# GELU MLP forward and backward on one core: a quarter of the slope's columns moved from VectorE to GpSimd in the first block

## Chip, core and metric

The kernel runs on one core of one Trainium2 chip. The metric is the device time of one launch in microseconds. A core has TensorE (matrix products, PE in the profile), VectorE (DVE), ScalarE (ACT), GpSimd (POOL) and SyncE (SP, which here only issues DMAs). TensorE writes its products to PSUM; GpSimd works on SBUF alone here.

## What is computed

A two-layer MLP with the tanh form of GELU, and all its gradients. Shapes: 2048 tokens, D = 448, F = 1792, all bf16.

```python
def _fwd_reference(x, w1, b1, w2, b2):
    h = jnp.einsum("bsd,df->bsf", x, w1) + b1
    h = _gelu(h)                     # jax.nn.gelu(x, approximate=True)
    return jnp.einsum("bsf,fd->bsd", h, w2) + b2

def reference(x, w1, b1, w2, b2, grad_out):
    ...
    _out, _vjp = jax.vjp(_f, x, w1, b1, w2, b2)
    _grads = _vjp(grad_out)
    return (_out0, *[jnp.asarray(_g) for _g in _grads])
```

So there are six outputs: the forward result, and the gradients of x, w1, b1, w2 and b2.

## The kernel before

The work is cut into four blocks of 512 tokens, and each block into 7 steps; a step holds two tiles of 128 hidden columns (f) by 512 tokens, so most tiles are 128 partitions by 2 x 512. Step numbers g run on over the blocks: 0 to 6 are the first block. The order of all instructions is written out by hand (`tc.manual_schedule()`), and each engine takes its instructions in that order.

What one step does, by function:

- `M1` (L251) and `rest` (L262, L266): TensorE makes u = x·w1 for a later step into the PSUM tile x, and begins grad_out·w2ᵀ in the PSUM tile z; `M4` (L272) completes z.
- `act_copy` (L297, L298): ScalarE copies u + b1 to V in SBUF and makes A, its scaled square. `act_gelu` (L301) makes hT = GELU(u).
- `dve_first` (L396): VectorE makes B, the cubic argument of tanh, from A and V. `act_second` (L399): ScalarE makes t = tanh.
- `dve_second`: VectorE makes the slope factor. `dve_p` (L402) makes p = (A + C)·hT; `dve_rest` makes t + 1 (L406), p - 1/2 (L407) and t·(p - 1/2) into t (L408).
- `dve_gate` (L416): VectorE makes ghT = (t + 1)·z, reading z in PSUM.
- `grow` (L437): TensorE adds this step's products to the block's forward output, held in the PSUM tiles y and w.

V, A and B have one buffer each; t and p have two, taken in turn by steps. In the first block the loop is, per step g:

```python
        if g > 0:
            rest([g + 1], [(g, pair("z"))])
            M4(g)
            dve_gate(g)
        if g < NPAIR - 1:
            act_first(g + 1)
            dve_first(g + 1)
            act_second(g + 1)
            dve_second(g + 1)
            grow(g, range(2 if g == 0 else 0, SPB))
            M1(g + 2, pair("x"))
            continue
```

`act_first` is `act_copy` and `act_gelu`. The slope of step 0 is made elsewhere, in two halves, by `first_chain` (its p and p - 1/2 are L359 and L361, with 512 columns). After step 6 the block's forward output is evicted, by ScalarE from y (L464) and by VectorE from w (L466), and the two PSUM tiles go to the next M1 and to the products of the next stage. From step 7 on the steps come in pairs, mixed with longer rows of products (L437).

SP issues the loads. w2ᵀ comes by DMA transposes in pieces of 256 columns; the last piece (`load_w2T(1536, F)`) can't be read with the usual overhang, so it comes in two transposes (L168, L169), and GpSimd copies 64 partitions of it into place (L170); columns 1536 on are first read in step 6. `end_in` does the same for grad_out's last rows, and `load_x` (L162) for those of x. Further, GpSimd issues the DMAs that store hT (L420) and the evicted outputs (L442), and at the end makes two sums over partitions (L602, L613).

Of the kernel before, what the change touches and what calls it, by code (L numbers as in the profile page):

```python
# [9 lines left out]
ALU = mybir.AluOpType  # L10
BF16 = mybir.dt.bfloat16
F32 = mybir.dt.float32

GELU_A = 0.044715
GELU_C = math.sqrt(2.0 / math.pi)
# [3 lines left out]
def kernel(  # L19
# [15 lines left out]
    nc = tc.nc  # L35
    P = 128
    B, S, D = x.shape
    F = w1.shape[1]
# [4 lines left out]
    KF = KD - 1  # L43
    DL = D - KF * P
    DOV = D - P
    DM = KF * P
    SB = 512
    NB = S // SB
    SPB = SB // P
    NPAIR = NF // 2  # L50
# [10 lines left out]
    const = ctx.enter_context(tc.tile_pool(name="const", bufs=1))  # L61
# [9 lines left out]
    def pair(name):  # L71
        return (psum_z if name == "z" else psum_s).tile([P, 2, SB], F32, name=name)
# [17 lines left out]
    B_flat = const.tile([P, 2 * SB], F32, name="Bt")  # L90
    T_flat = const.tile([P, 4 * 2 * SB], BF16, name="T")
    b2_bc = const.tile([P, D], BF16, name="b2_bc")
    b1_col = const.tile([P, NF], F32, name="b1_col")
    w128 = const.tile([P, P], BF16, name="w128")

    w1_sb = w1_flat.rearrange("p (k f) -> p k f", k=KD)
    w2T_sb = w2T_flat.rearrange("p (k f) -> p k f", k=KD)
# [8 lines left out]
    def xq(b):  # L106
        o = (b % 2) * 2 * KD * SB
        return xg_flat[:, o:o + KD * SB].rearrange("p (k s) -> p k s", k=KD)

    def gq(b):  # L110
        o = ((b % 2) * 2 + 1) * KD * SB
        return xg_flat[:, o:o + KD * SB].rearrange("p (k s) -> p k s", k=KD)

    def ring(t, n, g):
        o = (g % n) * 2 * SB
        return t[:, o:o + 2 * SB].rearrange("p (h s) -> p h s", h=2)

    def hT(g):
        return ring(hT_flat, HR, g)
# [7 lines left out]
    def A_of(g):  # L127
        return VA_flat[:, 2 * SB:4 * SB].rearrange("p (h s) -> p h s", h=2)

    def B_of(g):  # L130
        return ring(B_flat, 1, g)

    def t_of(g):
        return ring(T_flat, 4, 2 * (g % 2))

    def p_of(g):
        return ring(T_flat, 4, 2 * (g % 2) + 1)
# [10 lines left out]
    def row0(b):  # L148
        return (b + 1) % NB * SB

    def turn_in(out, src, off):
        nc.sync.dma_start_transpose(out=out, in_=bass.AP(src.tensor, src.offset + off, [src.ap[0], [1, KD * P]]))
# [11 lines left out]
    def end_in(dst, src, wrap):  # L164
        if wrap:
            turn_in(dst, src, 0)
        else:
            nc.sync.dma_start_transpose(out=dst[:, KF, :], in_=src[:, DOV:D])  # L168
            nc.sync.dma_start_transpose(out=dst[:, 0:KF, :], in_=src[:, 0:DM])  # L169
            nc.gpsimd.tensor_copy(out=dst[0:DL, KF, :], in_=dst[DL:P, KF, :])  # L170

    def load_g(b, r0=0, r1=SB):
        end_in(gq(b)[:, :, r0:r1], g2[row0(b) + r0:row0(b) + r1, :], row0(b) + SB < S)

    def load_w2T(f0, f1):
        end_in(w2T_sb[:, :, f0:f1], w2[f0:f1, :], f1 < F)
# [22 lines left out]
    for k in range(7):  # L199
        nc.vector.tensor_scalar(out=number[:, 1 << k:2 << k], in0=number[:, 0:1 << k], scalar1=float(1 << k), scalar2=None,  # L200
                                op0=ALU.add)
    for i in range(P // 32):
        nc.vector.transpose(out=row[32 * i:32 * (i + 1), :], in_=number[0:32, 32 * i:32 * (i + 1)])
    nc.vector.tensor_tensor(out=ident.rearrange("p (a b) -> p a b", b=32), in0=number.rearrange("p (a b) -> p a b", b=32),
                            in1=row[:, None, :].to_broadcast([P, P // 32, 32]), op=ALU.is_equal)
# [6 lines left out]
    load_w2(0, 2)  # L212
    load_w1(nc.sync, 256, 512)
    load_g(0, 0, HB)
    load_g(0, HB, SB)
    load_w1(nc.sync, 512, 768)
    load_w2T(256, 512)
# [22 lines left out]
    def cols(g, h):  # L240
        c = g % NPAIR
        return slice((2 * c + h) * P, (2 * c + h + 1) * P)
# [4 lines left out]
    def M1(g, u, hs=(0, 1)):  # L247
        u_of[g] = [u[:, h, :] for h in range(2)]
        for h in hs:
            for kt in range(KF):  # L250
                nc.tensor.matmul(u_of[g][h], lhsT=w1_sb[:, 1 + kt, cols(g, h)], rhs=xq(g // NPAIR)[:, 1 + kt, :],  # L251
                                 start=(kt == 0), stop=False, skip_group_check=True)

    def rest(us, qs):

        for gg, q in qs:
            g_of[gg] = q
        for i in range(2 * max(len(us), len(qs))):
            n, h = divmod(i, 2)
            if n < len(us):  # L260
                gu = us[n]
                nc.tensor.matmul(u_of[gu][h], lhsT=w1_sb[DL:P, 0, cols(gu, h)], rhs=xq(gu // NPAIR)[DL:P, 0, :],  # L262
                                 start=False, stop=True, tile_position=(DL, 0), skip_group_check=True)
            if n < len(qs):
                gg, q = qs[n]
                nc.tensor.matmul(q[:, h, :], lhsT=w2T_sb[0:DL, KF, cols(gg, h)], rhs=gq(gg // NPAIR)[0:DL, KF, :],  # L266
                                 start=True, stop=False, tile_position=(0, 0), skip_group_check=True)

    def M4(g):
        for h in range(2):  # L270
            for kt in range(KF):
                nc.tensor.matmul(g_of[g][:, h, :], lhsT=w2T_sb[:, kt, cols(g, h)], rhs=gq(g // NPAIR)[:, kt, :],  # L272
                                 start=False, stop=(kt == KF - 1), skip_group_check=True)
# [19 lines left out]
    def act_copy(g):  # L293
        u = u_of.pop(g)
        for h in range(2):
            ft = 2 * (g % NPAIR) + h
            nc.scalar.activation(out=V_of(g)[:, h, :], in_=u[h], func=ACT.Identity, bias=b1_col[:, ft:ft + 1])  # L297
        nc.scalar.activation(out=A_of(g), in_=V_of(g), func=ACT.Square, scale=math.sqrt(3.0 * GELU_C * GELU_A))  # L298

    def act_gelu(g):  # L300
        nc.scalar.activation(out=hT(g), in_=V_of(g), func=ACT.Gelu_apprx_tanh)  # L301

    def act_first(g):
        act_copy(g)
        act_gelu(g)
# [89 lines left out]
    def dve_first(g):  # L395
        nc.vector.scalar_tensor_tensor(out=B_of(g), in0=A_of(g), scalar=3.0 * GELU_C, in1=V_of(g), op0=ALU.add, op1=ALU.mult)  # L396

    def act_second(g):
        nc.scalar.activation(out=t_of(g), in_=B_of(g), func=ACT.Tanh, scale=-1.0 / 3.0)  # L399

    def dve_p(g):
        nc.vector.scalar_tensor_tensor(out=p_of(g), in0=A_of(g), scalar=GELU_C, in1=hT(g), op0=ALU.add, op1=ALU.mult)  # L402


    def dve_rest(g):
        nc.vector.tensor_scalar(out=t_of(g), in0=t_of(g), scalar1=1.0, scalar2=None, op0=ALU.add)  # L406
        nc.vector.tensor_scalar(out=p_of(g), in0=p_of(g), scalar1=-0.5, scalar2=None, op0=ALU.add)  # L407
        nc.vector.tensor_tensor(out=t_of(g), in0=t_of(g), in1=p_of(g), op=ALU.mult)  # L408

    def dve_second(g):  # L410
        dve_p(g)
        dve_rest(g)

    def dve_gate(g):
        q = g_of.pop(g)
        nc.vector.scalar_tensor_tensor(out=ghT(g), in0=t_of(g), scalar=1.0, in1=q[:], op0=ALU.add, op1=ALU.mult)  # L416
# [30 lines left out]
    def grow(g, js):  # L447
        for j in js:
            if g == 0 and j % 2 == 0:
                grown[j] = pair("yw"[j // 2])  # L450
            for h in range(2):
                product(grown[j - j % 2][:, j % 2, 0:D], "o", 0, j, 2 * g + h, j < 2)
# [8 lines left out]
    def evict_two(kind, b, j, t, by_act=False):  # L461
        st = iop.tile([P, 2, D], BF16, name="io_" + kind)
        if kind == "g" or by_act:
            nc.scalar.copy(out=st[:], in_=t[:, :, 0:D])  # L464
        else:
            nc.vector.tensor_tensor(out=st[:], in0=t[:, :, 0:D], in1=b2_bc[:, None, :].to_broadcast([P, 2, D]), op=ALU.add)  # L466
        send(kind, b, j, st)
# [23 lines left out]
    for g in range(NPAIR):  # L491
# [8 lines that stand above are left out]
            dve_second(g + 1)  # L500
            grow(g, range(2 if g == 0 else 0, SPB))
            M1(g + 2, pair("x"))
            continue

        grow(g, range(2))
        for j in range(2):
            nc.tensor.matmul(grown[0][:, j, 0:D], lhsT=w128[:], rhs=b2_bc[:], start=False, stop=True)
        grow(g, range(2, SPB))
        act_copy(g + 1)
        evict_two("o", 0, 0, grown[0], True)  # L510
        act_gelu(g + 1)
        dve_first(g + 1)
        act_second(g + 1)
        dve_p(g + 1)
        evict_two("o", 0, 2, grown[2])
        dve_rest(g + 1)
# [101 lines left out]
    def bank():  # L618
        nonlocal turn
        turn += 1  # L620
        return pair("ywxz"[turn % 4])[:, 0, :]
# [3 lines left out]
    for t0, t1 in ((0, 4), (4, HT)):  # L625
        n = (t1 - t0) * P
        for h in range(2):
            a0, a1 = t0 + h * HT, t1 + h * HT
            cs = slice(a0 * P, a1 * P)
            for kt in range(KF):  # L630
                ps = bank()
# [6 lines left out]
        ps = bank()  # L638
# [6 lines left out]
        for h in range(2):  # L645
            nc.scalar.dma_start(out=out_2[KF * P:D, (t0 + h * HT) * P:(t1 + h * HT) * P],
                                in_=gw1_rem[h * DL:(h + 1) * DL, t0 * P:t1 * P])


    for ft in range(NF):  # L650
        ps = bank()
# [41 lines left out]
```

## Time and profile before

| | us |
|---|---|
| median of three runs | 274.11 (273.96 to 274.13) |
| the profiled execution | 273.92 |
| its span | 272.2 |
| busy in the span: TensorE | 266.2 (98%) |
| VectorE | 193.6 (71%) |
| ScalarE | 143.4 (53%) |
| GpSimd | 53.7 (20%) |

The busy shares are means over stages with different limits. A matmul's end is modelled in the trace, so a busy TensorE can still have been held up. TensorE's granted clock was 1.0 over the whole span. The span is split into 40 equal slices of 6.8 us; in the first block, slices 2 to 7, VectorE shows 8 or 9 tenths busy and GpSimd nearly nothing:

```profile
DVE  5899999989889997889999885399999900000000
ACT  2988889798768677886868760012112121111111
POOL 0000001140513515113030415117000096000000
```

### The profile page before, as it was taken

To read this page: it belongs to the slowest core of one execution; us is meant where nothing else is said; L and a number is where in the kernel's file an instruction comes from. 1 tells how busy PE (TensorE), PEld (TensorE's weight loads), DVE (VectorE), ACT (ScalarE), POOL (GpSimd) and SP (SyncE) were. 2 spreads that over 40 slices of the span, in tenths; PEclk is the share of its full clock that TensorE was granted. 3 is DMA by queue.
4 is the path that set the end of the run, shared out by engine and by line. 5 is a ranking of instruction groups with operands and counts; after the bars stand their busy time and mean duration, and the time that the engine had idled before them with its cause. 6 is when DMAs were issued, how large, how long until landed. Compare 5 with 4: busy or idle time off the path is not lost.

```text
span 272.2 us, 3581 instructions
## 1 busy us (share of the span) xinstructions
PE 266.2 (98%) x1397; PEld 126.9 (47%) x1411; DVE 193.6 (71%) x235; ACT 143.4 (53%) x184; POOL 53.7 (20%) x59
## 2 busy tenths in 40 slices
PE   8999999999999999999999999999999999999995
PEld 3544434544444454444544454554445655555552
DVE  5899999989889997889999885399999900000000
ACT  2988889798768677886868760012112121111111
POOL 0000001140513515113030415117000096000000
PEclk9999999999999999999999999999999999999999
DMA  7999899921729999576332994999999911101110
GB/s 170 197 272 216 156 211 156 268 71 42 215 53 252 182 229 301 139 194 149 78 112 55 237 318 121 300 258 213 166 256 259 192 59 58 53 0 51 53 51 34
DMA packets 100445, 43.52 MB, mean 160 GB/s; under 512 B 89004, under 2 KB 97068, under 8 KB 100428
## 3 DMA queue, kind: packets, MB, share of 16 engines
q1 hardware_dynamic: 93344, 26.65, 51.3%
q0 software_dynamic: 4512, 14.69, 16.4%
q10 hardware_dynamic: 2572, 1.95, 2.3%
q8 instruction: 11, 0.18, 0.3%
q14 instruction: 6, 0.05, 0.1%
HBM read 7.00 MB, written 14.23 MB: 78 GB/s over the span
## 4 chain that ended last, share of the span: by engine, by line
PE 77%; DVE 14%; ACT 6%; DMA 2%; issue 1%; DVEq 0%
PE z L437 18%; PE z L272 5%; PE z L653 4%; PE y L653 4%; PE w L634 4%; PE w L272 4%; PE x L437 4%; PE y L437 4%; PE y L251 4%; PE x L634 3%; PE x L251 3%; PE w L653 3%; PE x L653 3%; PE y L634 3%; DVE ghT_h L416 3%; DVE Bt L396 3%
## 5 line engine op out<-in xcount | busy, mean ns | idle before, releaser
L399 ACT ACTIVATE T<-Bt 128x1024 bf16<-128x1024 f32 x27 | 28.5, 1057 | 16.9 <-DVE Bt L396 16.9
L396 DVE SCALAR_TENSOR_TENSOR Bt<-VA 128x1024 f32<-128x1024 f32 x27 | 33.1, 1226 | 0.9 <-ACT VA L298 0.8
L402 DVE SCALAR_TENSOR_TENSOR T<-VA,hT_h 128x1024 bf16<-128x1024 f32 x27 | 32.9, 1217 | 0.0
L437 PEld LDWEIGHTS <-ghT_h 128*128 128x128 bf16 x224 | 21.9, 98 | 21.0 <-issue 0.4
L437 PEld LDWEIGHTS <-hT_h 128*128 128x128 bf16 x224 | 21.8, 98 | 20.8 <-issue 0.2
L612 DVE TENSOR_TENSOR VA<-VA,gh_nat 128x1792 f32<-128x1792 f32 x14 | 30.0, 2142 | 0.5
L298 ACT ACTIVATE VA<-VA 128x1024 f32<-128x1024 f32 x27 | 28.5, 1057 | 0.9
L301 ACT ACTIVATE hT_h<-VA 128x1024 bf16<-128x1024 f32 x27 | 28.1, 1041 | 0.0
L437 PE MATMUL z<-w1T_gw,ghT_h 128*128 128x448 bf16 x140 | 27.3, 352 | 0.1
L634 PEld LDWEIGHTS <-w_x 128*128 128x128 bf16 x192 | 18.7, 98 | 17.8 <-issue 0.4
L297 ACT ACTIVATE VA<-x,b_col 128x512 f32<-128x512 f32 x34 | 21.4, 680 | 8.6 <-PE x L262 8.5
L416 DVE SCALAR_TENSOR_TENSOR ghT_h<-T,z 128x1024 bf16<-128x1024 bf16 x17 | 20.7, 1220 | 6.0 <-PE z L272 5.3
L272 PE MATMUL z<-xg_h,w2T_g 128*128 128x512 bf16 x101 | 24.7, 381 | 0.2 <-issue 0.2
L272 PEld LDWEIGHTS <-w2T_g 128*128 128x128 bf16 x162 | 14.5, 98 | 22.3 <-issue 7.2
L251 PE MATMUL x<-xg_h,w_x 128*128 128x512 bf16 x89 | 23.8, 379 | 0.7
L251 PEld LDWEIGHTS <-w_x 128*128 128x128 bf16 x162 | 15.7, 98 | 18.6 <-issue 0.7
L437 PE MATMUL z<-w_gw,hT_h 128*128 128x448 bf16 x112 | 22.0, 352 | 0.0
L420 POOL DMA_DIRECT2D hT_dram<-hT_h x28 | 20.2, 725 | 0.0
L408 DVE TENSOR_TENSOR T<-T 128x1024 bf16<-128x1024 bf16 x27 | 18.7, 693 | 0.9
L442 POOL DMA_DIRECT2D out_dram<-io_o x8 | 6.0, 750 | 62.4 <-DVE io_o L466 46.7
L442 POOL DMA_DIRECT2D out_dram<-io_g x8 | 5.8, 725 | 55.6 <-ACT io_g L464 55.6
L613 POOL PARTITION_ALL_REDUCE T<-VA x1 | 10.4, 10426 | 27.0 <-DVE VA L612 27.0
(117 smaller groups left out, 361.6 us busy)
## 6 DMA issues: line engine op xcount, KB each, us to landing
hT_dram<-hT_h POOLq DMA_DIRECT2D x28, 256.0 KB, 3.9
out_dram<-io_o POOLq DMA_DIRECT2D x8, 224.0 KB, 3.9
out_dram<-io_g POOLq DMA_DIRECT2D x8, 224.0 KB, 4.4
w_x<-in_x_dram POOLq DMA_DIRECT2D x1, 1344.0 KB, 9.1
w2T_g<-in_grad_out_dram POOLq DMA_DIRECT2D x1, 1344.0 KB, 7.6
out_dram<-w_gw SPq DMA_DIRECT2D x4, 336.0 KB, 2.4
w_x<-in_w_dram SPq DMA_DIRECT2D x2, 384.0 KB, 4.1
out_dram<-w1T_gw ACTq DMA_DIRECT2D x2, 384.0 KB, 4.6
```

What stands on the lines that cost most here:

```text
L251: nc.tensor.matmul(u_of[g][h], lhsT=w1_sb[:, 1 + kt, cols(g, h)], rhs=xq(g // NPAIR)[:, 1 + kt, :], start=(kt == 0), stop=False, skip_grou ...
L272: nc.tensor.matmul(g_of[g][:, h, :], lhsT=w2T_sb[:, kt, cols(g, h)], rhs=gq(g // NPAIR)[:, kt, :], start=False, stop=(kt == KF - 1), skip_ ...
L298: nc.scalar.activation(out=A_of(g), in_=V_of(g), func=ACT.Square, scale=math.sqrt(3.0 * GELU_C * GELU_A))
L301: nc.scalar.activation(out=hT(g), in_=V_of(g), func=ACT.Gelu_apprx_tanh)
L396: nc.vector.scalar_tensor_tensor(out=B_of(g), in0=A_of(g), scalar=3.0 * GELU_C, in1=V_of(g), op0=ALU.add, op1=ALU.mult)
L399: nc.scalar.activation(out=t_of(g), in_=B_of(g), func=ACT.Tanh, scale=-1.0 / 3.0)
L402: nc.vector.scalar_tensor_tensor(out=p_of(g), in0=A_of(g), scalar=GELU_C, in1=hT(g), op0=ALU.add, op1=ALU.mult)
L416: nc.vector.scalar_tensor_tensor(out=ghT(g), in0=t_of(g), scalar=1.0, in1=q[:], op0=ALU.add, op1=ALU.mult)
L437: nc.tensor.matmul(out, lhsT=lhsT, rhs=rhs, start=(ft == 0), stop=(ft == NF - 1 and not bias))
L612: nc.vector.tensor_tensor(out=gsb_v, in0=gsb_v, in1=gh_rows(st, 0, NF), op=ALU.add)
L634: nc.tensor.matmul(psv, lhsT=x_all[:, st, kt * P:(kt + 1) * P], rhs=gh_rows(st, a0, a1), start=(st == 0), stop=(st == NS - 1))
L653: nc.tensor.matmul(ps[:, 0:D], lhsT=h_blk[ft][:, st, :], rhs=g_all[:, st, :], start=(st == 0), stop=(st == NS - 1))
```

## The change

In steps 1 to 6, the last 128 of each 512 columns of p, (A + C)·hT - 1/2, are made by GpSimd in three instructions: A + C into a new float32 tile `sum_g`, the product with hT, and the subtraction of 1/2. VectorE makes the other 384 columns as before, and in these steps subtracts the 1/2 from p ahead of adding 1 to t. t·(p - 1/2) is still one VectorE instruction over all columns. From step 7 on, and in step 0, nothing changes.

The GpSimd copy of w2ᵀ's last piece is no longer issued with the loads, ahead of the first step, but in the loop at g = 4, behind `dve_second(5)`: in GpSimd's queue it stands behind the three instructions of step 5 and ahead of those of step 6. The copy for grad_out keeps its place. In the built program one more instruction stands in GpSimd's queue, ahead of the first sum: it loads a library of operations, as one does ahead of the first sum over partitions (L602) in both kernels.

```diff
+    sum_g = const.tile([P, 2, P], F32, name="sum_g")
...
             nc.sync.dma_start_transpose(out=dst[:, KF, :], in_=src[:, DOV:D])
             nc.sync.dma_start_transpose(out=dst[:, 0:KF, :], in_=src[:, 0:DM])
-            nc.gpsimd.tensor_copy(out=dst[0:DL, KF, :], in_=dst[DL:P, KF, :])
+
+    def end_copy(dst):
+        nc.gpsimd.tensor_copy(out=dst[0:DL, KF, :], in_=dst[DL:P, KF, :])
 
     def load_g(b, r0=0, r1=SB):
         end_in(gq(b)[:, :, r0:r1], g2[row0(b) + r0:row0(b) + r1, :], row0(b) + SB < S)
+        if row0(b) + SB == S:
+            end_copy(gq(b))
...
+    def dve_cols(g):
+        return slice(0, SB - P if g < NPAIR else SB)
+
     def dve_p(g):
-        nc.vector.scalar_tensor_tensor(out=p_of(g), in0=A_of(g), scalar=GELU_C, in1=hT(g), op0=ALU.add, op1=ALU.mult)
+        cs = dve_cols(g)
+        if g < NPAIR:
+            ps = slice(SB - P, SB)
+            nc.gpsimd.tensor_scalar(out=sum_g[:], in0=A_of(g)[:, :, ps], scalar1=GELU_C, scalar2=None, op0=ALU.add)
+            nc.gpsimd.tensor_tensor(out=p_of(g)[:, :, ps], in0=sum_g[:], in1=hT(g)[:, :, ps], op=ALU.mult)
+            nc.gpsimd.tensor_scalar(out=p_of(g)[:, :, ps], in0=p_of(g)[:, :, ps], scalar1=-0.5, scalar2=None, op0=ALU.add)
+        nc.vector.scalar_tensor_tensor(out=p_of(g)[:, :, cs], in0=A_of(g)[:, :, cs], scalar=GELU_C, in1=hT(g)[:, :, cs],
+                                       op0=ALU.add, op1=ALU.mult)
...
     def dve_rest(g):
-        nc.vector.tensor_scalar(out=t_of(g), in0=t_of(g), scalar1=1.0, scalar2=None, op0=ALU.add)
-        nc.vector.tensor_scalar(out=p_of(g), in0=p_of(g), scalar1=-0.5, scalar2=None, op0=ALU.add)
+        def on_t():
+            nc.vector.tensor_scalar(out=t_of(g), in0=t_of(g), scalar1=1.0, scalar2=None, op0=ALU.add)
+
+        def on_p():
+            ps = p_of(g)[:, :, dve_cols(g)]
+            nc.vector.tensor_scalar(out=ps, in0=ps, scalar1=-0.5, scalar2=None, op0=ALU.add)
+
+        for op in (on_p, on_t) if g < NPAIR else (on_t, on_p):
+            op()
         nc.vector.tensor_tensor(out=t_of(g), in0=t_of(g), in1=p_of(g), op=ALU.mult)
...
             M1(g + 2, pair("x"))
+            if g == NPAIR - 3:
+                end_copy(w2T_sb[:, :, 1536:F])
             continue
```

## The prediction

> **What bounds it now.** I read the page first (shares of the chain that ended last), then that chain in order of time over the first 60 us, then the timeline around it. Over the whole span the chain is mostly TensorE:
>
> ```profile
> PE 77%; DVE 14%; ACT 6%; DMA 2%; issue 1%; DVEq 0%
> ```
>
> In the stretch that the change touches it isn't. The chain in order of time (start, us, what) shows one step of the first block, and how it leaves the block:
>
> ```profile
> 14.42 1.22 DVE Bt L396
> ...
> 35.00 1.13 DVE Bt L396
> 36.13 1.14 DVE T L402
> 37.27 0.41 DVE T L406
> 37.68 0.35 DVE T L407
> 38.05 0.70 DVE T L408
> 38.85 1.22 DVE ghT_h L416
> 40.07 1.13 DVE Bt L396
> ...
> 42.77 0.69 ACT VA L297
> 43.48 1.06 ACT VA L298
> 44.53 0.79 ACT io_o L464
> ```
>
> From 14.42 to 42.77 every piece is VectorE: cubic (L396), p (L402), t+1 (L406), p-1/2 (L407), t*p (L408), gate (L416), 5.07 us a step, with no gap that another engine fills. TensorE's own pace is 4.75: its step starts (L262) are at 15.44, 20.18, 24.93 and 29.68 while it still has a lead, then at 34.74 and 39.81, held by VectorE. So VectorE time saved or added here moves the block's end. Behind step 6 ScalarE passes it on: its eviction of y (L464) ends at 45.33 and TensorE's next M1 starts at 45.38. From about 61 us the chain is almost all TensorE, so a shift at 45.38 goes through to the end.
>
> **What VectorE loses.** The groups by form give means:
>
> ```profile
> L402 DVE SCALAR_TENSOR_TENSOR T<-VA,hT_h 128x1024 bf16<-128x1024 f32 x27 | 32.9, 1217 | 0.0
> L406 DVE TENSOR_SCALAR T<-T 128x1024 bf16<-128x1024 bf16 x27 | 11.5, 426 | 3.0 <-ACT T L399 2.9
> L359 DVE SCALAR_TENSOR_TENSOR T<-VA,hT_h 128x512 bf16<-128x512 f32 x2 | 1.4, 683 | 0.0
> L361 DVE TENSOR_SCALAR T<-T 128x512 bf16<-128x512 bf16 x2 | 0.6, 294 | 0.1
> ```
>
> 512 columns less save 0.534 us in p and 0.132 in p-1/2; the change takes 256 (two halves of 128) off each: 0.27 + 0.07 = 0.33 a step in steps 1 to 6. VectorE alone would then need 5.07 - 0.33 = 4.74. Turning t+1 and p-1/2 round removes nothing, but covers the wait for tanh: in step 6 p ends at 42.34 and tanh (L399) at 42.29; with p 0.27 shorter t+1 would wait about 0.2, and p-1/2 now fills that.
>
> **What GpSimd adds.** Three instructions a step, on 256 columns each: sum (A + C), product (times h), minus 1/2. None of these is in the trace; the nearest rows are its copies, and they show what happens to VectorE next to them (start, us, engine, line):
>
> ```profile
> 29.58 0.39 POOL L170 COPY w2T_g<-w2T_g 64x256 bf16<-64x256 bf16 x1 [29.15 <-DMA w2T_g<-in_w_dram]
> ```
>
> ```profile
> 29.63 1.42 DVE L396 SCALAR_TENSOR_TENSOR Bt<-VA 128x1024 f32<-128x1024 f32 x1
> ```
>
> ```profile
> 58.46 0.43 DVE L406 TENSOR_SCALAR T<-T 128x1024 bf16<-128x1024 bf16 x1 [0.34 <-ACT T L399]
> 58.80 0.83 DVE L407 TENSOR_SCALAR T<-T 128x1024 bf16<-128x1024 bf16 x1
> ```
>
> ```profile
> 58.49 0.85 POOL L170 COPY xg_h<-xg_h 64x512 bf16<-64x512 bf16 x1
> ```
>
> Beside the first copy, which ends at 29.97, the cubic takes 1.42 instead of 1.22. Beside the second, which ends at 59.34, p-1/2 takes 0.83 instead of 0.42, and ends 0.29 behind the copy; the third copy, at 92.31, does the same (0.84). So a VectorE instruction with SBUF operands stands still until the GpSimd instruction is over, less some 0.14 of its start-up: 29.97 + 1.22 - 0.14 = 31.05, and 59.34 + 0.42 - 0.14 = 59.62, are the ends seen. And a GpSimd instruction that asked at 58.49, while L406 ran, got in ahead of the next VectorE instruction. Each GpSimd instruction next to a back-to-back VectorE thus costs its own length less 0.14.
>
> Lengths: sum and minus 1/2 read 256 elements, as the 0.39 copy: 0.39 (upper end 0.43, half the 512 copy). The product reads 2 x 256: between 0.39 and the 512 copy's 0.86, of which up to 0.4 may have been waiting for L406; I take the middle of 0.45 and 0.86, 0.65. [...]
>
> Where each falls. The square (L298) ends 4.56 behind its step's cubic start (34.91 to 39.47), and the gate then still runs, to 40.07. The gate's second operand is in PSUM, and I take it that the sum runs beside it for nothing: it would end at about 39.9, before the cubic. If the gate is held too, the sum costs 0.25 a step. [...] The product is released by GELU (L301), which ends 5.50 behind the previous cubic: at the next cubic's start or just behind it, so it gets in before p and holds p for 0.65 - 0.14 = 0.51. Minus 1/2 follows and gets in behind p: 0.39 - 0.14 = 0.25. Net per step: 0.51 + 0.25 - 0.33 = +0.43; the step becomes 5.50. In step 1 sum and cubic are both released by the square that ends at 14.39, with no gate beside them: +0.25 once.
>
> How many steps count: tanh(6), copy(7) and the eviction that TensorE waits for hang on cubic(6), so what is put behind cubics 1 to 5 arrives, 5 x 0.43 = 2.15. Step 6's own is covered: gate(6) ends at 45.14, and TensorE's z group that it frees starts at 46.77. Sum: 2.15 + 0.25 = +2.4.
>
> **New waits.** t*p now waits for GpSimd (the gate, and TensorE's z group, stand behind it); GpSimd is done some 3.2 us into the step and t*p is due at about 3.8, so 0.6 covers it. The square waits for the sum of the step before, over 3 us earlier. GpSimd's queue: a library load stands ahead of the first sum; GpSimd is otherwise idle until 14.4, and the reduction that follows such a load in the trace (L602, 4.38 us with all) is far shorter than that, so nothing. w2T's last copy left its place at the head of the queue, where sum(1) would have stood behind its DMA until 29.5. It now stands behind minus 1/2 of step 5, near 40, and is needed by TensorE's L266 of step 6, at 40.12 + 2.2 = 42.3: covered by 2 us, and beyond that TensorE would wait for all the rest. It holds VectorE for about as much (0.25) as it did at 29.63 (0.20): nothing. The out DMA behind it (45.64) shifts with the rest. SP's transposes keep their order.
>
> **Time.** The profiled execution took 273.92 (span 272.2): 273.92 + 2.4 = 276.3. The median shown, 274.11, is 0.19 above it: 276.5.
>
> **Rivals.**
> - *Faster: GpSimd runs beside VectorE almost free.* If only that first start-up is disturbed, VectorE's 4.74 goes below TensorE's 4.75, which then sets the pace. M1 of step 3 at 28.29 would be followed at 33.04, 37.79 and (0.38 more for the bias products) 42.92, in place of 43.84; then M1 on y at 44.2 in place of 45.38. That is 0.9 to 1.2 less, 273.0. For it: GpSimd is idle there, and the cubic lost only 0.20 of a 0.39 copy. Against it: three copies, three delays of 0.2 to 0.42. It decides where product and minus 1/2 together hold VectorE by less than 0.33.
> - *About the same.* Both instructions short, near 0.3 each: 0.16 + 0.16 - 0.33 = 0, 274.1. Against: the shortest row is 0.39, on half the partitions.
> - *Slower still: VectorE doesn't let GpSimd in.* Its instructions overlap by 0.08 or so, so GpSimd may get in only where t*p makes VectorE wait: 0.65 + 0.39 and 0.1 for two hand-overs, less 0.33: +0.81 a step, 5 x 0.81 = +4.1, 278.2. The order at 58.49 speaks against it.
>
> **Chances and range.** Forecast 0.54, let in last 0.14, same 0.10, faster 0.22. A difference under 0.2%, 0.55 us, can't be told from none; the forecast's lower end lies above that. Its own ends: product and minus 1/2 at 0.39 each give +0.17 a step, 0.85 in all, 274.9; product 0.86, minus 1/2 0.43 and the sum not hidden give 0.72 + 0.29 + 0.25 - 0.33 = 0.93, 4.9 in all, 279.0. To hold 8 in 10 the range has to take in the faster case as well: 272.9 to 279.0. Slower 0.54 + 0.14 = 0.68.
>
> **What would show it.** In the profile after: p at 0.95 plus a hold where the product runs; cubics 5.3 to 5.7 apart in the first block; p or p-1/2 stretched beside each GpSimd row; M1 on y near 47.7. I'm wrong if the cubics come 4.75 apart, if VectorE's rows keep their lengths beside GpSimd's, or if t*p shows a wait for GpSimd (the third rival). If GpSimd's product is nearer 1 us than 0.65, only the size is off.

## The result and the profile after

The changed kernel takes 276.34 us (median of six, 276.13 to 276.89) beside 274.01 for the kernel before: a ratio of 1.0095, interval 1.0084 to 1.0106. The profiled execution took 276.47, with a span of 274.7 in place of 272.2. All ratios in this document are of fast executions; the kernel below with fewer columns has one slow one, of 717.44 us, which is in its median but not in its ratio.

The chain that ended last, in order of time (start, us, what), is again VectorE through the whole first block, now with GpSimd at its head (most pieces of a step are left out here; they are in the timeline below):

```profile
14.13 1.90 POOL sum_g L414
16.11 0.79 POOL T L415
16.98 0.94 POOL T L416
17.94 0.70 DVE T L432
...
36.62 1.14 DVE Bt L401
37.76 1.36 DVE T L417
...
42.22 1.14 DVE Bt L401
```

A step (cubic L401 to cubic) is 5.60 where it was 5.07 (steps 3 to 6; steps 1 and 2 are 5.81 and 5.47). p (L417), on fewer columns, stays longer in the chain than before: 1.36 where L402 had 1.14. The page's shares say the same from far off (VectorE 14% before):

```profile
PE 76%; DVE 15%; ACT 4%; DMA 2%; POOL 1%; issue 1%; DVEq 0%
```

Further on in the chain, TensorE's long row of products behind the gate of step 8, before and after:

```profile
61.55 5.46 PE z L437 x28
```

```profile
64.10 5.46 PE z L461 x28
```

VectorE's instructions of step 5 in the timeline (start, us, engine, line) show where the time sits:

```profile
35.40 1.22 DVE L440 SCALAR_TENSOR_TENSOR ghT_h<-T,z 128x1024 bf16<-128x1024 bf16 x1
36.54 1.22 DVE L401 SCALAR_TENSOR_TENSOR Bt<-VA 128x1024 f32<-128x1024 f32 x1
37.68 1.43 DVE L417 SCALAR_TENSOR_TENSOR T<-VA,hT_h 128x768 bf16<-128x768 f32 x1
39.14 0.43 DVE L428 TENSOR_SCALAR T<-T 128x768 bf16<-128x768 bf16 x1
39.50 0.61 DVE L424 TENSOR_SCALAR T<-T 128x1024 bf16<-128x1024 bf16 x1
40.21 0.69 DVE L432 TENSOR_TENSOR T<-T 128x1024 bf16<-128x1024 bf16 x1
```

and GpSimd's instructions in the same stretch, with step 2's product above them:

```profile
19.76 0.67 POOL L415 TENSOR_TENSOR T<-sum_g,hT_h 128x256 bf16<-128x256 f32 x1 [0.15 <-POOL sum_g L414]
...
35.63 0.85 POOL L414 TENSOR_SCALAR sum_g<-VA 128x256 f32<-128x256 f32 x1 [1.40 <-ACT VA L303]
36.63 1.66 POOL L415 TENSOR_TENSOR T<-sum_g,hT_h 128x256 bf16<-128x256 f32 x1 [0.15 <-POOL sum_g L414]
38.38 1.45 POOL L416 TENSOR_SCALAR T<-T 128x256 bf16<-128x256 bf16 x1
39.89 0.46 POOL L173 COPY w2T_g<-w2T_g 64x256 bf16<-64x256 bf16 x1
```

In what follows an instruction is held by as much as its row is longer than its free length, which is its length with no GpSimd instruction beside it (0.95 for p and 0.36 for p-1/2 on these columns, from the kernel below with nothing on GpSimd). The product asks at 36.63, just behind the cubic's start, and ends at 38.29. p starts at 37.68, and ends at 39.11: 38.29 + 0.95 - 0.14 = 39.10, the prediction's arithmetic. So p is held 0.48. In step 2 the product came ahead of the cubic and took 0.67 with nobody in its way; there the product held the cubic (1.64) in place of p, and minus 1/2 held p by 0.19 (1.14). In steps 3 to 6 minus 1/2 (L416) costs p-1/2 (L428, 0.43 for a free 0.36) 0.07 and t+1 (L424, 0.61 for 0.42) 0.19. The sum runs 0.85 beside the gate, and neither the gate nor the cubic behind it is longer than 1.22.

### The profile page after: what moved, and what is told of

Same layout as the page of the kernel before. It is cut to its first block, busy times and chain, and to the rows that moved or that the text cites. A ratio compares the mean times of both kernels' runs of the same rounds, so it can differ in the third digit from the quotient of the medians.

```text
span 274.7 us, 3615 instructions
## 1 busy us (share of the span) xinstructions
PE 266.5 (97%) x1397; PEld 126.7 (46%) x1411; DVE 195.5 (71%) x235; ACT 143.4 (52%) x184; POOL 75.5 (27%) x77
## 4 chain that ended last, share of the span: by engine, by line
PE 76%; DVE 15%; ACT 4%; DMA 2%; POOL 1%; issue 1%; DVEq 0%
PE z L461 17%; PE z L277 5%; PE z L679 4%; PE y L679 4%; PE w L660 4%; PE w L277 4%; PE y L461 4%; PE x L461 4%; PE y L256 4%; DVE ghT_h L440 4%; PE x L660 3%; PE x L256 3%; PE x L679 3%; PE w L679 3%; DVE T L417 3%; PE y L660 3%
## 5 line engine op out<-in xcount | busy, mean ns | idle before, releaser
L401 DVE SCALAR_TENSOR_TENSOR Bt<-VA 128x1024 f32<-128x1024 f32 x27 | 33.3, 1235 | 0.9 <-ACT VA L303 0.8
L417 DVE SCALAR_TENSOR_TENSOR T<-VA,hT_h 128x1024 bf16<-128x1024 f32 (+1 forms) x27 | 33.6, 1244 | 0.0
```

The source lines that it names most:

```text
L417: nc.vector.scalar_tensor_tensor(out=p_of(g)[:, :, cs], in0=A_of(g)[:, :, cs], scalar=GELU_C, in1=hT(g)[:, :, cs], op0=ALU.add, op1=ALU.mult)
```

## Experiments

Theory: VectorE stands still while GpSimd's instruction works on SBUF beside it, so the change costs the holds less the columns saved. The rival then still open: the cost is in the waiting that the change wrote into the program (t*p and the square wait for GpSimd, p-1/2 stands directly behind p).

For each profiled execution, the starts of the cubics of steps 1 and 7 and the span, with the median and the ratio to before on the same chip (there before had medians of 273.85 for the four kernels under after, 273.82 for the next four, 273.49 for the next two and 273.63 for the last two):

| kernel | cubic 1 | cubic 7 | span | span less cubic 7 | median | ratio (interval) |
|---|---|---|---|---|---|---|
| before | 14.42 | 45.05 | 272.2 | 227.2 | 274.01 | |
| after | 14.06 | 47.74 | 274.7 | 227.0 | 276.34 | 1.0095 (1.0084 to 1.0106) |
| GpSimd beside, nobody waits | 13.98 | 48.27 | 275.3 | 227.0 | 277.13 | 1.0124 (1.0109 to 1.0139) |
| fewer columns, no GpSimd | 14.55 | 43.76 | 271.2 | 227.4 | 273.01 | 0.9960 (0.9945 to 0.9975) |
| copy moved alone | 14.37 | 44.83 | 271.9 | 227.1 | 273.69 | 1.0000 (0.9987 to 1.0013) |
| order turned back | 14.54 | 48.23 | 275.2 | 227.0 | 276.53 | 1.0101 (1.0084 to 1.0119) |
| sum alone beside | 14.02 | 44.84 | 272.0 | 227.2 | 273.75 | 1.0004 (0.9990 to 1.0018) |
| 64 columns | 14.09 | 46.14 | 273.1 | 227.0 | 274.89 | 1.0048 (1.0031 to 1.0065) |
| GpSimd without minus 1/2 | 14.28 | 45.92 | 272.9 | 227.0 | 274.79 | 1.0049 (1.0030 to 1.0069) |
| A in bf16 | 14.71 | 45.27 | 272.4 | 227.1 | 273.91 | 1.0002 (0.9991 to 1.0013) |
| A + C first | 14.11 | 46.22 | 273.3 | 227.1 | 275.62 | 1.0075 (1.0062 to 1.0088) |
| ScalarE half | 14.10 | 45.54 | 272.6 | 227.1 | 274.93 | 1.0049 (1.0036 to 1.0062) |
| ScalarE half, turned | 14.07 | 43.60 | 271.1 | 227.5 | 273.19 | 0.9982 (0.9972 to 0.9993) |
| ScalarE half, plain | 14.45 | 44.40 | 271.7 | 227.3 | 273.36 | 0.9988 (0.9978 to 0.9997) |

From cubic 7 to the end every execution needs 227.0 to 227.5: the span is set by when step 7 begins. Where that is earlier than in before, up to 0.3 of the lead is lost behind it (227.4 and 227.5 in the two earliest). The start of cubic 1 differs by up to 0.7 from profile to profile and goes into the span too.

**GpSimd's work beside the kernel before.** The three instructions write to a scratch tile; VectorE does all it did before, in the old order.

```diff
-            nc.gpsimd.tensor_tensor(out=p_of(g)[:, :, ps], in0=sum_g[:], in1=hT(g)[:, :, ps], op=ALU.mult)
-            nc.gpsimd.tensor_scalar(out=p_of(g)[:, :, ps], in0=p_of(g)[:, :, ps], scalar1=-0.5, ...)
+            nc.gpsimd.tensor_tensor(out=side_g[:], in0=sum_g[:], in1=hT(g)[:, :, ps], op=ALU.mult)
+            nc.gpsimd.tensor_scalar(out=side_g[:], in0=side_g[:], scalar1=-0.5, ...)
...
-        return slice(0, SB - P if g < NPAIR else SB)
+        return slice(0, SB)
```

> GpSimd's three instructions of steps 1 to 6 write to a scratch tile that nothing reads; VectorE makes all 512 columns of p in the order of before, so it saves nothing and waits for nothing new. Hold theory (a VectorE instruction with SBUF operands stands still until the GpSimd instruction beside it is over): p loses about 0.48 to the product and the two instructions behind it about 0.26 to minus 1/2, so cubics 5.8 apart in place of 5.07, and 5 to 6 such steps: 278.0 to 278.6. Wait theory (the cost of the change is that t*p and the square now wait for GpSimd): 274.0, cubics 5.07 apart.

Measured 277.13, 3.3 above before: under the forecast of the hold theory, and far from the 274.0 of the wait theory. The steps alternate: 5.87, 5.57, 5.86, 5.57, 5.93, 5.49. VectorE's rows of a short and a long step:

```profile
31.28 1.59 DVE L402 SCALAR_TENSOR_TENSOR Bt<-VA 128x1024 f32<-128x1024 f32 x1
32.79 1.41 DVE L418 SCALAR_TENSOR_TENSOR T<-VA,hT_h 128x1024 bf16<-128x1024 f32 x1
34.13 0.41 DVE L425 TENSOR_SCALAR T<-T 128x1024 bf16<-128x1024 bf16 x1
...
37.98 1.69 DVE L418 SCALAR_TENSOR_TENSOR T<-VA,hT_h 128x1024 bf16<-128x1024 f32 x1
39.60 0.61 DVE L425 TENSOR_SCALAR T<-T 128x1024 bf16<-128x1024 bf16 x1
40.13 0.61 DVE L429 TENSOR_SCALAR T<-T 128x1024 bf16<-128x1024 bf16 x1
```

Where the product came ahead of the cubic (at 31.12, the cubic at 31.28), cubic and p lose 0.37 and 0.19; where it came behind (at 37.35, the cubic at 36.85), p, t+1 and p-1/2 lose 0.47, 0.19 and 0.19. The same work lengthens VectorE's rows by 0.56 or 0.85, and the step by 0.50 or 0.79, depending on which engine was first. No VectorE instruction depends on GpSimd here, and none of VectorE's rows up to 50 us shows a wait for it, so the hold is shown and the wait theory falls. Cubic 1 to cubic 7 grew by 3.66; 0.44 of that is hidden in this profile by its early start.

**Fewer columns, nothing on GpSimd.** Columns 384 to 511 of each 512 of p are left unmade in steps 2 to 6.

```diff
-            nc.gpsimd...   (all three)
-        return slice(0, SB - P if g < NPAIR else SB)
+        return slice(0, SB - P if 2 <= g < NPAIR else SB)
```

> Steps 2 to 6 leave the last 128 of each 512 columns of p unmade (they keep older values), nothing runs on GpSimd for them, and p-1/2 stands ahead of t+1 as after. Hold theory: VectorE really saves 0.33 a step, its 4.74 falls to TensorE's 4.75, and the block ends 0.9 to 1.2 earlier: 272.8 to 273.2. If the saving is eaten by fixed costs of the instructions or by the new order (p-1/2 directly behind p): cubics still near 5.0 apart, 273.8 to 274.1.

Measured 273.01, ratio 0.996. Steps are 4.78 to 4.79 (4.99 where w2T's copy held p by 0.20). VectorE thus saves 0.28, not 0.33: p-1/2 starts 0.99 behind p, whose free length is 0.95, while in the kernel before the next instruction starts 0.02 ahead of p's end. p and p-1/2 of step 5:

```profile
35.32 0.95 DVE L411 SCALAR_TENSOR_TENSOR T<-VA,hT_h 128x768 bf16<-128x768 f32 x1
36.31 0.36 DVE L422 TENSOR_SCALAR T<-T 128x768 bf16<-128x768 bf16 x1
```

This is what the change would be worth, over five of its six steps, if GpSimd's part were free, and it is the time of the prediction's faster rival.

**The copy alone.** The kernel before with `end_copy` in its new place.

> Before, with only w2T's last copy moved behind step 5. Hold theory: the copy held step 4's cubic for 0.20 and now falls where it holds little or nothing: 273.8 to 274.1. Wait theory: the copy is late for step 6 and TensorE waits for it: over 274.3.

Measured 273.69, 0.1 under the first forecast, ratio 1.000. With nothing else on GpSimd the copy ran when its DMA landed, as before (at 29.27; before, at 29.58), this time inside the gate, and held nothing, so neither theory was put to the test: the place in the queue would matter only with other GpSimd work in front (after, the copy ran at 39.89, behind minus 1/2).

**The order of t+1 and p-1/2 turned back.**

```diff
-        for op in (on_p, on_t) if g < NPAIR else (on_t, on_p):
+        for op in (on_t, on_p):
```

> After, with t+1 again ahead of p-1/2. Hold theory: since the product already holds p past the end of tanh, the turned order covers nothing any more; turning it back takes away the back-to-back dependence of p-1/2 on p (some 0.05 a step) and leaves the holds: 275.9 to 276.4. If the order still covers a wait for tanh (0.2 a step, as the prediction had it for VectorE alone): 277.0 to 277.5.

Measured 276.53, ratio 1.0101 beside 1.0095: no difference that can be told, 0.1 above the first forecast and well under the second. The steps are 5.60 again: the 0.05 between p and p-1/2 goes, but t+1 (0.61) and p-1/2 (0.54 for 0.36) now lose 0.19 each to minus 1/2.

**The sum alone, beside the kernel before.**

```diff
-            nc.gpsimd.tensor_tensor(...)      (product)
-            nc.gpsimd.tensor_scalar(...)      (minus 1/2)
...
+        return slice(0, SB)
```

> GpSimd makes only its first instruction, the sum, in steps 1 to 6, into a tile that nothing reads; VectorE makes all of p as before. Alone the sum took 0.85, and it starts when the square ends, 4.6 behind the cubic; so in a step of 5.07 it runs 0.8 beside or behind the gate and reaches 0.39 into the next cubic. Hold theory: the gate (second operand in PSUM) isn't held, the cubic is, by 0.39 less 0.14: cubics 5.3 apart, 275.0 to 275.6. If any GpSimd instruction held any VectorE instruction, the gate too: 0.7 a step, 277 to 278. If the sum doesn't hold: 273.9.

Measured 273.75, ratio 1.0004. The forecast of 275 missed; the last case came. The GpSimd row, then VectorE's gate and cubic:

```profile
34.18 0.85 POOL L414 TENSOR_SCALAR sum_g<-VA 128x256 f32<-128x256 f32 x1 [4.22 <-ACT VA L303]
```

```profile
33.43 1.22 DVE L438 SCALAR_TENSOR_TENSOR ghT_h<-T,z 128x1024 bf16<-128x1024 bf16 x1
34.57 1.22 DVE L401 SCALAR_TENSOR_TENSOR Bt<-VA 128x1024 f32<-128x1024 f32 x1
```

The gate is free, as forecast. But the sum's record reaches to 35.03, 0.46 into the cubic, and the cubic is not held. In step 1, where both begin together at 14.0, the cubic takes 1.47, held 0.25. By these rows the sum holds only during its first 0.4 (the 0.25, and the 0.14 that a held row here doesn't lose, as in 38.29 + 0.95 - 0.14 = 39.10 above). What GpSimd does in the rest of the 0.85 was not separated, and its start and end are known only from its record.

**64 columns in place of 128.**

```diff
-        return slice(0, SB - P if g < NPAIR else SB)
+        return slice(0, SB - 64 if g < NPAIR else SB)
...
-            ps = slice(SB - P, SB)
+            ps = slice(SB - 64, SB)
```

> After, with 64 of each 512 columns on GpSimd in place of 128. Hold theory with lengths that go by columns: VectorE saves half, 0.14 with what p-1/2 behind p costs, and loses half of 0.48 and of 0.26, and the same 0.07 at t*p: steps of 5.35 to 5.4, 275.2 to 275.8. If GpSimd's lengths are mostly fixed: 0.14 saved, 0.74 + 0.07 lost, steps of 5.7, 277 to 278.

Steps 5.34, as columns go; 274.89 is 0.3 under the forecast. p loses 0.24, t+1 0.09. A smaller share costs less, but is still a loss.

**GpSimd without minus 1/2.** VectorE subtracts 1/2 from all columns, behind t+1.

```diff
-            nc.gpsimd.tensor_scalar(out=p_of(g)[:, :, ps], in0=p_of(g)[:, :, ps], scalar1=-0.5, ...)
...
-            ps = p_of(g)[:, :, dve_cols(g)]
+            ps = p_of(g)
```

> After, but GpSimd makes only sum and product of its 128 columns; VectorE subtracts 1/2 from all 512, behind t+1. Hold theory: the 0.26 that minus 1/2 holds go, 0.07 come back for the wider p-1/2: steps of 5.35 to 5.45 in place of 5.60, 275.2 to 275.8. If the cost sat in t*p's wait for GpSimd rather than in the holds, the product's end would now be waited for at p-1/2 and nothing would change: 276.3.

Steps 5.20 and 5.21 (5.41 in step 1 and in step 5, where the copy held t+1 by 0.21), 274.79: lower than forecast. p keeps its hold of 0.48; t+1 and p-1/2 are back at 0.41. So minus 1/2 was worth 0.39 of the 0.53, more than the 0.26 seen on its two neighbours: with it go also the dependence on p of the instruction behind it (p-1/2 started 0.03 behind p's end, t+1 here starts 0.07 ahead of it) and t*p's second wait (0.06).

**Versions without GpSimd.** VectorE's time is the price, so I cut it in other ways. In all but the last, p in steps 1 to 6 becomes A + C, from an A that ScalarE writes in bf16, and a bf16 product; they differ in where A + C is made.

```diff
+            nc.vector.tensor_scalar(out=p_of(g), in0=A_of(g), scalar1=GELU_C, ..., op0=ALU.add)
+            nc.vector.tensor_tensor(out=p_of(g), in0=p_of(g), in1=hT(g), op=ALU.mult)
```

> Before, without GpSimd: in steps 1 to 6 ScalarE writes A in bf16, and VectorE makes p as two bf16 instructions, A + C (0.35 from start to start, as p-1/2) and the product with hT (0.70, as t*p), in place of one of 1.14. If VectorE's time sets the block, 0.09 a step: cubics 4.98 apart, 273.2 to 273.5. If it doesn't, 273.9; if two dependent instructions cost 0.05 more as p-1/2 behind p does, 273.6 to 273.8.

Nothing: the product starts 0.52 behind the A + C that it needs, and steps stay at 5.07. With A + C moved ahead of the cubic:

> The kernel with A in bf16 (no GpSimd), with A + C moved ahead of the cubic, so that the product no longer stands directly behind the instruction that it needs: that cost 0.52 from start to start where 0.35 was counted. If VectorE's time sets the block: A + C 0.35, cubic 1.14, product 0.70 in place of 1.14 + 0.53 + 0.68, cubics 4.95 to 5.0 apart, 273.2 to 273.5. If the cubic, now 0.35 later, holds ScalarE's round (tanh, copy, square, cubic: 4.6 + 0.35) and that becomes the bound: 4.95, the same. If nothing is gained: 273.9.

And with ScalarE making half of it:

```diff
     def act_second(g):
+        if 0 < g < NPAIR:
+            nc.scalar.activation(out=p_of(g)[:, :, HB:SB], in_=A_of(g)[:, :, HB:SB], func=ACT.Identity, bias=c_col[:, 0:1])
```

> The same, and ScalarE makes A + C of half the columns in the 0.8 that it waits between GELU and tanh; VectorE the other half ahead of the cubic. If VectorE's time sets the block and ScalarE's wait hides it: 0.21 + 1.14 + 0.70 in place of 2.28, cubics 4.8 to 4.9 apart, 272.8 to 273.2, as the kernel with fewer columns and no GpSimd. If ScalarE's instruction (0.57 to 0.62) comes late and pushes tanh: 273.5 to 274.

Both missed, and slower than before: 275.62 and 274.93, with steps of 5.41 and 5.27. Three lines of VectorE's timeline in the first of them say why:

```profile
24.92 1.22 DVE L401 SCALAR_TENSOR_TENSOR Bt<-A_half,VA 128x1024 f32<-128x1024 bf16 x1
26.06 0.69 DVE L408 TENSOR_TENSOR T<-T,hT_h 128x1024 bf16<-128x1024 bf16 x1
27.26 0.43 DVE L414 TENSOR_SCALAR T<-T 128x1024 bf16<-128x1024 bf16 x1 [0.52 <-ACT T L404]
```

t+1 waits 0.52 for tanh: it can't start less than 2.34 behind the cubic (24.92 to 27.26), and in the kernel before it starts 2.34 behind as well (34.91 to 37.25). There tanh ended at 37.22 and p at 37.27, so VectorE's busy time and the round cubic, tanh, t+1, t*p, gate were equal; work taken out between cubic and t+1 brings nothing unless something else moves in, and work put ahead of the cubic lengthens the round. So p-1/2 has to go ahead of t+1, which is what the change under study does:

> The kernel in which ScalarE makes A + C of half the columns, with p-1/2 ahead of t+1. The last two kernels showed that t+1 can't start before tanh ends, 2.34 behind the cubic's start, and that VectorE stood idle 0.5 there. If that is the round that sets a step (what stands between gate and cubic, 0.20; cubic and tanh 2.34; then t+1 0.45, t*p 0.80, gate 1.14), p-1/2 fits into the idle time: 4.93 in place of 5.27, 0.14 a step under before, 0.6 to 0.9 in all less than before. If the round isn't the bound and the turned order only shifts work: as the kernel without the turn, 1.3 above before.

And the plain form, with A in float32 again:

> Before, without bf16 A and with nothing between gate and cubic: in steps 1 to 6 ScalarE makes A + C of the last 256 of each 512 columns behind GELU, VectorE makes p of the first 256 as before (0.68) and multiplies the others by hT in bf16 (0.43), and p-1/2 stands ahead of t+1. By the round: t+1 at 1.13 + 0.60 + 0.37 + 0.33 = 2.43 behind the cubic, then 0.45, 0.80, 1.14: 4.82; ScalarE needs 4.25 + 0.62 = 4.87. So 4.82 to 4.9 a step, 0.2 under before, 0.8 to 1.2 in all less than before. If ScalarE's instruction pushes tanh late: 5.07 or more, no gain.

The turn alone takes the step from 5.27 to 4.94, and the time to 273.19, ratio 0.9982; the plain form has steps of 4.92 but one, of 5.34, and 0.9988. In that step the gate waited 0.52; the profile names only t*p, which had ended just as long before, so the cause stays open. Both beat the kernel before by less than the forecast, 0.3 to 0.5 us. Both intervals lie under 1, the second's by 0.0003 only.

## Why the prediction was right

The forecast was 276.5, the time measured 276.34, and the reason holds: VectorE is the path of the first block, and GpSimd's instructions hold it for longer than they relieve it. By its own steps:

- *The holds.* Product 0.51 forecast, 0.48 measured, and its length 0.65 forecast, 0.67 measured. Minus 1/2: 0.25 forecast, 0.07 + 0.19 = 0.26 measured, on p-1/2 and t+1 and not on one instruction. That this size was met is in part luck: the rule that VectorE stands until GpSimd's row ends, less 0.14, fits the copies and the product, but in step 2 minus 1/2 ran to 22.21 beside p, and p ended at 22.57 and not at 22.21 + 0.95 - 0.14 = 23.02.
- *The sum.* Mis-sized: 0.39 forecast, 0.85 measured. It didn't matter, since it fits beside the gate, which keeps its 1.22 in every kernel here. That the sum costs nothing beside the gate was assumed in the prediction, and no row of the kernel before shows it; the kernel with the sum alone does (the sum's 0.85 from 34.18, the gate's 1.22 from 33.43). There the cubic that ran 0.46 beside the sum's end kept its 1.22 as well, if GpSimd's record is taken at its word.
- *The saving.* 0.33 forecast, 0.28 measured without GpSimd: p-1/2 directly behind the p that it needs costs 0.05. And t*p, which now waits for two engines, starts 0.10 behind the end of t+1 where it started 0.04 behind its forerunner. The step became 5.60, forecast 5.50: 0.48 + 0.26 - 0.28 + 0.06 = 0.52, seen as +0.53, in place of +0.43.
- *How many steps count.* Here the prediction was wrong. It let step 6 be covered, since the M1 on y hangs on cubic 6, and that M1 did move by only 2.2 (45.38 to 47.59). But VectorE, with ScalarE between (56.52 to 60.99 in the chain after), carried step 6's delay through steps 7 and 8, and the gate of step 8, which ended at 61.50 before and at 64.06 after, held TensorE's next long row of products: from 61.55 to 64.10, 2.55 later. The chain of the kernel before already ran this way. The nearly constant 227 us behind cubic 7 shows six steps.
- *Why the sum still came out.* Cubic 1 to cubic 7 grew by 3.05 (30.63 to 33.68), not by 2.4; in that, step 4 of before had 0.20 from w2T's copy, which held nothing after, where the prediction let the copy cancel. But the profiled execution of after began its first cubic 0.36 earlier, at 14.06. That looks like chance, though one profile of each kernel can't show it: the start lies between 13.98 and 14.71 over the fourteen profiles, 14.54 in the kernel with the order turned back, whose span is 3.0 above before. And 0.13 is taken back at p of step 7, which before waited for GELU (46.32, 1.27 behind its cubic; after, 48.87, 1.13 behind). For the two profiles that is 3.05 - 0.36 - 0.13 = 2.56, the 2.5 of their spans. Without the early start it is 2.9, the upper end of what the ratio allows (2.3 to 2.9). So the cost a step and the count of steps were both forecast too low, and that the time came within 0.2 of the forecast is partly luck.
- *Step 1.* 0.25 forecast for sum against cubic; the cubic came first, and the sum held p by 0.20 (1.15). Step 1 was 5.81, with t*p waiting 0.28 for GpSimd, the only such wait.
- *The rivals.* VectorE that doesn't let GpSimd in would show t*p waiting in each step: it waits once. GpSimd almost free would leave the lengths beside it alone; but its time, 273.0, is what the kernel without GpSimd took. w2T's copy ran at 39.89, ahead of its need at 42.28, and held nothing.
- *The range.* Its lower end, 274.9, leaves out the 0.25 of step 1 that the upper end has in; with it, it would be 275.2.

The prediction had the wait for tanh as the reason for the new order (about 0.2 in step 6). What it did not say, and the kernels without GpSimd show, is that cubic, tanh, t+1, t*p and gate make a round as long as VectorE's busy time, so that this busy time alone does not give the step.

## What to carry to other kernels

Look at where work handed to GpSimd will run. Here VectorE paid for it, in part or in full, beside its instructions with all operands in SBUF (in steps 3 to 6, 0.48 a step for the product and 0.26 for minus 1/2), and it was free beside the gate, whose second operand is in PSUM (1.22 with the sum's 0.85 beside it and without; that PSUM is the reason was not shown); so hand over what is ready there and fits. Before shortening the busiest engine, find the round that it waits for: here t+1 never started less than 2.34 behind the cubic, whatever stood between, and without GpSimd the shorter work counted only with the order changed (steps of 5.27 in the old order, 4.94 in the new). And count the steps that a delay passes by following it to the point where the bounding engine next waits, not to the first hand-over.

## What the runs showed of the hardware

GpSimd's record of the two instructions with a constant (sum, minus 1/2) is longer than their hold: of the float32 sum's 0.89 about 0.4 held the cubic (started together at 14.0 in the kernel with the sum alone, the cubic took 1.47, 0.25 more than its 1.22), and minus 1/2, with a record of 1.45 in steps 3 to 6, held p-1/2 by 0.07 and t+1 by 0.19. Where the copies and the product held a row, the hold lasted to the end of the record, less 0.14 (the product's at 38.29 held p to 39.11; the copy's at 59.34, in the kernel before, p-1/2 to 59.63). In the kernel with the order turned back minus 1/2 lengthened both bf16 instructions, t+1 (0.61 for 0.42) and p-1/2 (0.54 for 0.36), by 0.19 each; why is not shown. Beside the kernel before, VectorE's rows lost 0.56 a step to the same three instructions where the product came ahead of the cubic, and 0.85 where it came behind.
